# One operation for the three scalings of an attention step, and a newly drawn order of work

## The chip, the cores and the metric

The kernel runs on one core of one Trainium2 chip. The metric is the device time of one execution in microseconds (us), from launch to end. The core has five engines that run side by side: TensorE (PE in the rows; its weight loads are PEld), VectorE (DVE), ScalarE (ACT), GpSimd (POOL) and SyncE (SP), which issues the transfers. SBUF is the on-chip working memory, PSUM the memory into which TensorE writes.

## The reference, cut to what matters

Three stages follow one another: an attention over a sliding window of 64 positions, a feed-forward stage with a rational activation, and a second, bilinear feed-forward stage.

```python
# q, k, v: (4, 8, 576, 64)
scores = scale * np.matmul(q, k.transpose(0, 1, 3, 2))
scores = np.where((rel >= 0) & (rel < 64), scores, -1000000000.0)
attn = np.exp(scores - scores.max(-1, keepdims=True))
attn = attn / (np.sum(attn, axis=-1, keepdims=True) + 1e-09)   # the scaling
x = np.matmul(attn, v)            # then reshaped to (2304, 512)
h = x @ w_in                      # (512, 2048)
g = (a0 + a1*h + a2*h*h + a3*h*h*h) / (1 + |b0|*|h| + |b1|*h*h + 1e-6)
x = g @ w_out                     # (2048, 512)
out = ((x @ w1) * (x @ w2)) @ w3 @ w_out2
```

## The kernel before, in words

**The attention.** The work is cut into 48 steps. A step is one pair of heads and 192 query positions, in three windows of 64 positions; its scores fill a tile `sm` of 128 partitions by 3 x 128 elements. Two consecutive steps are a pair (the function `attn`) and share a small tile `st` of 24 columns, in which the row minima, the row sums, the sums plus 1e-9 and their reciprocals of both steps stand, three columns for each step. One step is this chain: the scores on TensorE (`S`, L555); for each of the three windows a masked row minimum on VectorE (`tr`, L558) and an exponential with row sum on ScalarE (`e`, L564); once for the pair, the sum plus 1e-9 on GpSimd (`rs`, L498) and the reciprocal on VectorE (`rc`, L501); for each window the scaling of the 128 x 128 block by its reciprocals (`nm`, on ScalarE at L569 or on GpSimd at L571); three transposes on TensorE (`T`, L576); one copy out of PSUM on ScalarE (`ac`, L581); the product with v on TensorE (`O`, L508); and once for the pair two operations that split the result into two tiles for the next stage (`xh` on ScalarE, L518; `xl` on VectorE, L521).

**The first feed-forward stage** takes blocks of 384 tokens. Its products are L646 (`hp`) and L723 (`acc`), its activation runs on ScalarE and VectorE, and the last multiplication of it, `lo` (L717), can run on VectorE or, for the first three blocks, on GpSimd. The weights arrive as 64-bit numbers and are converted by five operations each, four on VectorE (L408, L411, L414, L424) and one on ScalarE (L421). The second feed-forward stage (L1023, L1150 and L879) has no part in the attention's work.

**What sets the order.** No loop emits the instructions. Every operation is registered with the engines it may run on and a cost in us for each (`op`), with what it comes after and which buffers it uses; the costs are numbers written by hand. The planner (`order`, L72 to L216) lays all operations of the kernel out in one schedule by these costs and due times, 17 times over, and keeps the shortest one. The due times of the first round are shifted by random numbers from a seed (L198). Where an operation names two engines, the planner takes one of them. It lets an operation on GpSimd and one of VectorE that is marked `port=True` never overlap in its schedule. The order of the shortest schedule is the order of instructions on every engine and of the transfers in SyncE's queue. So a cost or the seed can move any instruction of the kernel.

Of the 48 steps, the first 16 may scale on GpSimd; the other 32 scale on ScalarE.

Of the kernel before, what the change touches and what calls it, by code (L numbers as in the profile page):

```python
# [3 lines left out]

# [36 lines left out]
class Plan:  # L41
# [30 lines left out]
    def order(self, rounds=16):  # L72
# [122 lines left out]

        first = dues(base)
        preds = buffers(lambda a: first[a] if ops[a]["turn"] is None else ops[a]["turn"])
        rng = Random(55)  # L198
        due = [d + rng.gauss(0.0, 0.5) for d in dues(preds)]
        best = None  # L200
        for r in range(rounds + 1):
# [18 lines left out]
def body(ctx: ExitStack, tc: tile.TileContext, qkv, qk0, w_in, w_out, a, b, w1, w2, w3t, wo2, out):  # L220
# [260 lines left out]
    def attn(pair):  # L481


        i0 = 2 * pair
        u, p0 = STEPS[i0]
        s = u % NU
        j, o = u // 2, (u % 2) * U
        early = i0 < 2 * NP
        y = units.setdefault(u, [{} for _ in range(NP // 2)])[p0 // 2]

        def rows(f):
            return y["st"][:, 6 * f:6 * f + 6]

        def col(f, k, m):
            return y["st"][:, 6 * f + NW * k + m:6 * f + NW * k + m + 1]

        def rs(_):
            nc.gpsimd.tensor_scalar(out=rows(2), in0=rows(1), scalar1=1e-9, scalar2=1.0, op0=ADD, op1=MUL)  # L498

        def rc(_):  # L500
            dve.reciprocal(rows(3), rows(2))  # L501

        def O(k, y=y):
            if k == 0:
                y["op"] = psum.tile([P, 2, U], F32, tag="at", bufs=2, name="op")
            for w in range(NW):
                for h in (slice(0, 64), slice(64, P)):
                    nc.tensor.matmul(y["op"][h, k, w * W_:(w + 1) * W_], y["v", k][:, w, h], y["ac", k][:, w, h], start=True, stop=True)  # L508
            if u % 2 == 0 and k == 0 and y is units[u][0]:
                xh[j], xl[j] = xtiles(XSLOT[j], "x")  # L510

        def OO(_):
            for y in units[u]:
                for k in range(2):
                    O(k, y)

        def xh_(_):
            act(xh[j][:, p0:p0 + 2, o:o + U], y["op"], cp)  # L518

        def xl_(_):  # L520
            dve.tensor_tensor(out=xl[j][:, p0:p0 + 2, o:o + U], in0=y["op"], in1=xh[j][:, p0:p0 + 2, o:o + U], op=SUB)  # L521

        def step(k):
            i, p = i0 + k, p0 + k

            tags = (f"acc{i % 2}", f"acc{2 + i % 2}") if early else ("at", "at")
            x = {}

            def load(_):
                x["k"] = ap_.tile([P, U + W_], F32, tag="k", bufs=rings["k"], name="k")  # L530
                if i < THIN:
                    if k == 0:
                        y["q"] = ap_.tile([P, 2 * U], F32, tag="q", bufs=rings["q"], name="q")
                        nc.sync.dma_start(out=y["q"], in_=qk0[u, p0 // 2])
                    x["q"] = y["q"].rearrange("d (k w n) -> d k w n", k=2, w=NW)[:, k]
                    nc.sync.dma_start(out=x["k"], in_=qkv[u, p, :, 2 * U:3 * U + W_])
                    return
                q = ap_.tile([P, 2 * U], F32, tag="q", bufs=rings["q"], name="q")
                x["q"] = q.rearrange("d (w n) -> d w n", w=NW)
                nc.sync.dma_start(out=q, in_=qkv[u, p, :, 0:2 * U])  # L540
                nc.sync.dma_start(out=x["k"], in_=qkv[u, p, :, 2 * U:3 * U + W_])

            def loadv(_):
                y["v", k] = ap_.tile([P, NW, P], F32, tag="v", bufs=rings["v"], name="v")
                nc.sync.dma_start(out=y["v", k], in_=qkv[u, p, :, 3 * U + W_:].rearrange("r (w d) -> r w d", w=NW))


            def S_(_):
                x["sp"] = sp = psum.tile([P, NW, P], F32, tag=tags[0], bufs=rings[tags[0]], name="sp")
                x["sm"] = ap_.tile([P, NW, P], F32, tag="sm", bufs=rings["sm"], name="sm")  # L550
                if k == 0:
                    y["st"] = ap_.tile([P, 24], F32, tag="st", bufs=rings["st"], name="st")
                for w in range(NW):
                    for h in (slice(0, 64), slice(64, P)) if i < THIN else (slice(0, P),):
                        nc.tensor.matmul(sp[h, w, :], x["q"][h, w], x["k"][h, w * W_:w * W_ + P], start=True, stop=True)  # L555

            def tr(m):
                dve.tensor_tensor_reduce(  # L558
                    out=x["sm"][:, m, :], in0=x["sp"][:, m, :], in1=mask0 if s == 0 and m == 0 else mask, scale=-SCALE, scalar=3.0e38,
                    op0=ADD, op1=ALU.min, accum_out=col(0, k, m),  # L560
                )

            def e(m):
                act(x["sm"][:, m, :], x["sm"][:, m, :], AF.Exp, bias=col(0, k, m), scale=-1.0, accum_out=col(1, k, m))  # L564

            def nm(m, e):
                r, t = col(3, k, m), x["sm"][:, m, :]
                if e == "A":
                    act(t, t, cp, scale=r)  # L569
                else:  # L570
                    nc.gpsimd.tensor_scalar(out=t, in0=t, scalar1=r, scalar2=1.0, op0=MUL, op1=MUL)  # L571

            def T(_):
                x["tp"] = tp = psum.tile([P, NW, P], F32, tag=tags[1], bufs=rings[tags[1]], name="tp")
                for w in range(NW):
                    nc.tensor.transpose(tp[:, w, :], x["sm"][:, w, :], idn)  # L576

            def ac(_):

                y["ac", k] = x["sm"]  # L580
                act(y["ac", k], x["tp"], cp)  # L581

            kb_, vb, qb, mb, sp, tp = ("k", i), ("v", i), ("q", i0 if i < THIN else i), ("sm", i), (tags[0], ("S", i)), (tags[1], ("T", i))
            thin = i < THIN
            op(("load", i), (("D", (0.48 if k else 1.12) if thin else 1.1),), load, after=[("load", i0)] if thin and k else (), new=(kb_,) if thin and k else (kb_, qb), uses=(qb,) if thin and k else (), tail=2.2)
            op(("loadv", i), (("D", 0.66),), loadv, after=(("load", i),), new=(vb,), tail=2.2)
            pe(("S", i), S_, TS, after=[("load", i)] + [("S", i - 1)] * k, new=(sp, mb) if k else (sp, mb, sb), uses=(kb_, qb, sb) if k else (kb_, qb))
            for m in range(NW):
                op(("tr", i, m), (("V", 0.21),), lambda _, m=m: tr(m), after=(("S", i),), uses=(sp, mb, sb))
                op(("e", i, m), (("A", 0.39),), lambda _, m=m: e(m), after=(("tr", i, m),), uses=(mb, sb))  # L590
            for m in range(NW):
                op(("nm", i, m), (("A", 0.32), ("P", 0.52)) if i < 16 else (("A", 0.32),), lambda e, m=m: nm(m, e), after=(("rc", i0),), uses=(sb, mb))
            pe(("T", i), T, TT, after=[("nm", i, m) for m in range(NW)], new=(tp,), uses=(mb,))
            op(("ac", i), (("A", 0.45),), ac, after=(("T", i),), uses=(tp, mb))
            if early:
                xn = i == 0
                pe(("O", i), lambda _: O(k), TO[k], after=[("ac", i), ("loadv", i)] + [("O", i - 1)] * k, new=() if k else (ob, xb) if xn else (ob,), uses=(mb, vb, ob, xb) if k else (mb, vb) if xn else (mb, vb, xb))

        sb, ob, xb = ("st", i0), ("at", ("O", i0)), (f"x{XSLOT[j]}", j)
        op(("rs", i0), (("P", 0.12),), rs, after=[("e", i0 + k, m) for k in range(2) for m in range(NW)], uses=(sb,))  # L600
        op(("rc", i0), (("V", 0.12),), rc, after=(("rs", i0),), uses=(sb,))
        for k in range(2):
            step(k)
        if not early and p0:
            four, xn = range(i0 - 2, i0 + 2), u % 2 == 0
            new = (("at", ("O", i0 - 2)), ob) + ((xb,) if xn else ())
            pe(("O", i0 + 1), OO, TOO, after=[(w, i) for i in four for w in ("ac", "loadv")], new=new, uses=tuple((b, i) for i in four for b in ("sm", "v")) + (() if xn else (xb,)))
        op(("xh", i0), (("A", 0.40),), xh_, after=(("O", (i0 if early else i0 // NP * NP + 2) + 1),), uses=(ob, xb))
        op(("xl", i0), (("V", 0.43),), xl_, after=(("xh", i0),), uses=(ob, xb))


    kept, AGAIN = {}, "again"
# [21 lines left out]
    def chunks(c0):  # L634
# [121 lines left out]
        op(("w", c0), (("V", 0.87),), w, port=True, after=(("hi", c0),), uses=(b["qa"], b["g"]))  # L756
        op(("d", c0), (("V", 0.87 if estrin else 0.93),), d, port=True, after=(("w", c0),), uses=(b["u"], b["qa"]))
        for m in range(2):
            engines = (("V", 0.47), ("P", 0.97))[:2 if j < G else 1]
            op(("lo", c0 + m), engines, lambda e, m=m: lo(m, e), port=True, after=(("d", c0),), uses=(b["u"], b["r"], b["g"]))  # L760
        for m in range(2):
            c, f = c0 + m, f0 + m
# [497 lines left out]
```

## Time and profile before

| what | us |
|---|---|
| median of 3 runs | 814.37 (813.99 to 817.33) |
| the profiled execution | 815.26 |
| span of its instructions | 813.4 |
| around the span | 1.9 |

A page of the profile has the busy time of each engine, a line of the span in 40 slices, the chain of work that ended last, and groups of instructions by source line. Tables by stretch give the busy time of each engine between two times; a table of waits says which engine's idle time ended with which other instruction; a timeline lists single instructions. The longest instruction of an engine is not its cost alone: an instruction that cannot get at its data shows the time as its own.

### The profile page before, as it was taken

The numbers are of one execution on the slowest core, as the hardware profiler recorded it, in microseconds if no ns is written. First come the engines' busy times: TensorE is split into PE (matmuls) and PEld (weight loads), VectorE is DVE, ScalarE is ACT, GpSimd is POOL, SyncE is SP. The second block draws the span as 40 slices with busy tenths as digits, with TensorE's granted clock in tenths as the row PEclk, the third lists the DMA queues.
The fourth block names the chain that finished last, engine by engine and source line by source line (L and its number), as shares of the span: only waits on it lengthen the run. The fifth ranks groups of instructions, "written<-read, shape, count | busy, mean of one in ns | idle before, by whom it ended". The sixth has DMA issues, their size and how long they took to land.

```text
span 813.4 us, 14381 instructions
## 1 busy us (share of the span) xinstructions
PE 789.3 (97%) x5112; PEld 767.6 (94%) x5112; DVE 734.0 (90%) x1445; ACT 562.6 (69%) x1263; POOL 47.0 (6%) x72
## 2 busy tenths in 40 slices
PE   5779999999999999999999999999999999999998
PEld 4579999999999999999999999889999999999998
DVE  6999999999999899999999999899999788837854
ACT  6998996787889878788877676267465456544433
POOL 2223210000001200000000000000000000000000
PEclk9999999999999999999999999999999999999999
DMA  8883473234438666455443632678978775136402
GB/s 279 296 280 116 118 228 117 98 97 144 149 120 269 215 207 208 161 204 184 145 140 137 241 120 85 213 255 280 330 243 268 240 269 177 63 116 213 160 1 77
DMA packets 62951, 147.74 MB, mean 182 GB/s; under 512 B 7072, under 2 KB 35744, under 8 KB 62880
## 3 DMA queue, kind: packets, MB, share of 16 engines
q1 hardware_dynamic: 62880, 146.83, 53.4%
q8 instruction: 40, 0.66, 0.3%
q14 instruction: 31, 0.25, 0.1%
HBM read 114.30 MB, written 32.51 MB: 180 GB/s over the span
## 4 chain that ended last, share of the span: by engine, by line
PE 85%; DVE 9%; DMA 3%; ACT 2%; issue 1%; POOL 0%; SPq 0%; DVEq 0%; POOLq 0%
PE acc L723 23%; PE hp L646 22%; PE pb L1023 8%; PE wp L879 5%; PE pc L1023 5%; PE pa L1023 5%; PE pb L1150 5%; PE pc L1150 3%; PE pa L1150 3%; PE sp L555 3%; PE op L508 2%; PE tp L576 1%; DVE wt L414 1%; DVE wt L411 1%; DMA wc<-kw 1%
## 5 line engine op out<-in xcount | busy, mean ns | idle before, releaser
L646 PE MATMUL hp<-x,wc 128*128 128x384 f32 x1152 | 218.9, 338 | 2.8 <-DVE u L674 2.1
L723 PE MATMUL acc<-g,wc 128*128 128x384 f32 x1152 | 219.4, 338 | 1.2 <-DVE g L717 1.1
L646 PEld LDWEIGHTS hp<-x,wc 128*128 128x128 f32 x1152 | 199.6, 188 | 5.2 <-DVE u L674 2.9
L723 PEld LDWEIGHTS acc<-g,wc 128*128 128x128 f32 x1152 | 199.6, 188 | 3.6 <-DVE g L717 2.4
L1023 PE MATMUL pb<-xb,wc 128*128 128x384 f32 x432 | 84.2, 334 | 0.0
L1023 PEld LDWEIGHTS pb<-xb,wc 128*128 128x128 f32 x432 | 75.7, 188 | 0.0
L687 ACT ACTIVATE r<-qa,cq 128x768 f32<-128x768 f32 x48 | 45.3, 943 | 41.0 <-DVE qa L683 23.1
L668 ACT ACTIVATE u<-hp,ca 128x384 f32<-128x384 f32 x96 | 65.0, 677 | 6.7 <-PE hp L646 6.4
L663 ACT ACTIVATE qa<-hp,cb 128x384 f32<-128x384 f32 x96 | 55.8, 581 | 13.1 <-PE hp L646 10.9
L564 ACT ACTIVATE sm<-sm,st 128x128 f32<-128x128 f32 x144 | 56.1, 399 | 9.1 <-DVE st L558 8.9
L1112 ACT ACTIVATE rt<-prod 128x768 fp32r<-128x768 f32 x42 | 35.5, 846 | 32.2 <-PE pb L1150 9.7
L1023 PE MATMUL pa<-xb,wc 128*128 128x384 f32 x288 | 56.9, 335 | 0.5 <-DMA wc<-kw 0.5
L1023 PE MATMUL pc<-xb,wc 128*128 128x384 f32 x288 | 55.9, 334 | 0.0
L555 PE MATMUL sp<-k,q 64*64 64x128 f32 (+1 forms) x384 | 42.9, 309 | 12.8 <-DMA k<-in_qkv 8.5
L1115 DVE TENSOR_TENSOR rt<-prod,rt 128x768 fp32r<-128x768 f32 x42 | 40.0, 955 | 16.5 <-ACT rt L1112 16.0
L658 ACT ACTIVATE h<-hp 128x384 f32<-128x384 f32 x96 | 47.1, 490 | 9.6 <-PE hp L646 7.9
L555 PEld LDWEIGHTS sp<-k,q 64*64 64x64 f32 (+1 forms) x384 | 39.0, 183 | 15.1 <-issue 8.3
L1023 PEld LDWEIGHTS pa<-xb,wc 128*128 128x128 f32 x288 | 50.5, 188 | 1.0 <-DMA wc<-kw 0.8
L1023 PEld LDWEIGHTS pc<-xb,wc 128*128 128x128 f32 x288 | 50.4, 188 | 0.0
L683 DVE SCALAR_TENSOR_TENSOR qa<-h,cab,qa 128x768 f32<-128x768 f32 x48 | 48.4, 1008 | 1.2 <-ACT qa L663 1.1
L411 DVE SCALAR_TENSOR_TENSOR wt<-ws,wt 128x512 uint32<-128x512 uint32 x72 | 49.0, 682 | 0.3
L414 DVE SCALAR_TENSOR_TENSOR wt<-ws,wt 128x512 uint32<-128x512 uint32 x72 | 49.0, 683 | 0.1
(86 smaller groups left out, 1376.9 us busy)
## 6 DMA issues: line engine op xcount, KB each, us to landing
wc<-kw SPq DMA_DIRECT2D x48, 512.0 KB, 4.9
bs<-kb SPq DMA_DIRECT2D x24, 512.0 KB, 4.3
v<-in_qkv SPq DMA_DIRECT2D x48, 192.0 KB, 3.9
ws<-in_w_in SPq DMA_DIRECT2D x16, 512.0 KB, 4.8
ws<-in_w_out SPq DMA_DIRECT2D x16, 512.0 KB, 4.8
ws<-in_w SPq DMA_DIRECT2D x16, 512.0 KB, 4.0
kw<-ws SPq DMA_DIRECT2D x16, 512.0 KB, 3.5
ws<-in_w3t SPq DMA_DIRECT2D x16, 512.0 KB, 4.1
```

The lines of the kernel that those rows point to most:

```text
L411: stt(out=x["b"], in0=x["st"][:, :, 0], scalar=29, in1=x["b"], op0=ALU.logical_shift_right, op1=ALU.bitwise_or)
L414: stt(out=x["b"], in0=x["st"][:, :, 1], scalar=0xC0000000, in1=x["b"], op0=ALU.bitwise_and, op1=ALU.bitwise_or)
L555: nc.tensor.matmul(sp[h, w, :], x["q"][h, w], x["k"][h, w * W_:w * W_ + P], start=True, stop=True)
L564: act(x["sm"][:, m, :], x["sm"][:, m, :], AF.Exp, bias=col(0, k, m), scale=-1.0, accum_out=col(1, k, m))
L646: nc.tensor.matmul(x["hp", m], win[f0 + m][:, s_, kk * P:(kk + 1) * P], (xh, xl)[m_][xk][:, kk, :], start=(kk == 0 and i == 0), stop=(kk = ...
L658: act(x["h2"][:, m, :], x["hp", m], AF.Square)
L663: act(x["qa"][:, m, :], x["hp", m], AF.Abs, scale=b0)
L668: act(x["u"][:, m, :], x["hp", m], AF.Identity, scale=a3, bias=a2)
L683: stt(out=x["qa"], in0=x["h2"], scalar=b1, in1=x["qa"], op0=MUL, op1=ADD)
L723: nc.tensor.matmul(accs[j, part, n], wout[f0 + m][:, s_, n * P:(n + 1) * P], x["g"][:, m_, m, :], start=(first and i == 0), stop=(last and ...
L1023: nc.tensor.matmul(x[m], sws[u, n, i0][:, s_, (c0 + k) * P:(c0 + k + 1) * P], t[:, m_, k, :], start=(first and k == 0 and i == 0), stop=(k ...
L1150: nc.tensor.matmul(x[m, n], w[:, s_, (c + n) * P:(c + n + 1) * P], rts[u, b, r][:, m_, k, :], start=(first and r == 0 and k == 0 and i == ...
```

## The change

In the first 16 steps the three scalings `nm` of a step become one operation `nms`. On GpSimd it is a single multiplication of the whole tile by the three reciprocals, each spread over its 128 columns; on ScalarE it is the same three instructions as before, one behind the other, but taken or left as a whole. Some costs that the planner reckons with are changed as well (`rs`, `ac`, `xh`, `xl`, and `lo` on GpSimd), and the seed.

```diff
-        rng = Random(55)
+        rng = Random(19)
...
+            def nms(e):
+                if e == "A":
+                    for m in range(NW):
+                        nm(m, e)
+                else:
+                    r = y["st"][:, 18 + NW * k:18 + NW * (k + 1)].unsqueeze(2).to_broadcast([P, NW, P])
+                    nc.gpsimd.tensor_tensor(out=x["sm"], in0=x["sm"], in1=r, op=MUL)
...
-            for m in range(NW):
-                op(("nm", i, m), (("A", 0.32), ("P", 0.52)) if i < 16 else (("A", 0.32),), lambda e, m=m: nm(m, e), after=(("rc", i0),), uses=(sb, mb))
-            pe(("T", i), T, TT, after=[("nm", i, m) for m in range(NW)], new=(tp,), uses=(mb,))
-            op(("ac", i), (("A", 0.45),), ac, after=(("T", i),), uses=(tp, mb))
+            whole = i < 2 * 2 * NP
+            for m in range(0 if whole else NW):
+                op(("nm", i, m), (("A", 0.32),), lambda e, m=m: nm(m, e), after=(("rc", i0),), uses=(sb, mb))
+            if whole:
+                op(("nm", i), (("A", 0.9), ("P", 1.25)), nms, after=(("rc", i0),), uses=(sb, mb))
+            pe(("T", i), T, TT, after=[("nm", i)] if whole else [("nm", i, m) for m in range(NW)], new=(tp,), uses=(mb,))
+            op(("ac", i), (("A", 0.43),), ac, after=(("T", i),), uses=(tp, mb))
...
-        op(("rs", i0), (("P", 0.12),), rs, after=[("e", i0 + k, m) for k in range(2) for m in range(NW)], uses=(sb,))
+        op(("rs", i0), (("P", 0.3),), rs, after=[("e", i0 + k, m) for k in range(2) for m in range(NW)], uses=(sb,))
...
-        op(("xh", i0), (("A", 0.40),), xh_, after=(("O", (i0 if early else i0 // NP * NP + 2) + 1),), uses=(ob, xb))
-        op(("xl", i0), (("V", 0.43),), xl_, after=(("xh", i0),), uses=(ob, xb))
+        op(("xh", i0), (("A", 0.43),), xh_, after=(("O", (i0 if early else i0 // NP * NP + 2) + 1),), uses=(ob, xb))
+        op(("xl", i0), (("V", 0.465),), xl_, after=(("xh", i0),), uses=(ob, xb))
...
-            engines = (("V", 0.47), ("P", 0.97))[:2 if j < G else 1]
+            engines = (("V", 0.47), ("P", 1.4))[:2 if j < G else 1]
```

## Rows read from the trace of the kernel before

**Rows 1.** The page, busy time of each engine, share of the span, instructions:

```profile
PE 789.3 (97%) x5112; PEld 767.6 (94%) x5112; DVE 734.0 (90%) x1445; ACT 562.6 (69%) x1263; POOL 47.0 (6%) x72
```

**Rows 2.** Table by stretch: busy us of each engine, granted clock, DMA share, GB/s:

```profile
0.00:14.00 14.00, 5.46 (x47) 4.72 (x49) 7.86 (x32) 6.30 (x22) 2.27 (x13) 1.00 0.79 262
14.00:76.00 62.00, 51.75 (x517) 45.19 (x516) 58.98 (x169) 55.82 (x174) 21.29 (x31) 0.97 0.72 246
76.00:470.00 394.00, 392.66 (x2666) 386.73 (x2663) 388.48 (x773) 320.92 (x755) 23.44 (x29) 1.00 0.50 167
470.00:814.00 344.00, 339.44 (x1895) 330.98 (x1893) 278.67 (x473) 179.58 (x316) 0.00 (x0) 1.00 0.54 183
```

**Rows 3.** Waits in 14:76: us in total, times, longest us:

```profile
PEld op L508 <- ACT sm L581: 3.2, 5, 1.1
PEld hp L646 <- DVE u L674: 2.4, 1, 2.4
PEld sp L555 <- DVE x L521: 2.4, 1, 2.4
...
PEld tp L576 <- POOL sm L571: 1.4, 2, 0.9
...
PEld tp L576 <- ACT sm L569: 0.6, 1, 0.6
```

**Rows 4.** Groups by line, 14:76: count, busy us, mean ns, idle before:

```profile
L571 POOL TENSOR_SCALAR sm<-sm,st 128x128 f32<-128x128 f32 x19 | 12.5, 670 | 7.3 <-DVE st L501 7.3
L717 POOL TENSOR_TENSOR g<-u,r 128x384 fp32r<-128x384 f32 x5 | 6.9, 1397 | 10.5 <-ACT x L518 6.1 <-DVE u L713 4.5
...
L569 ACT ACTIVATE sm<-sm,st 128x128 f32<-128x128 f32 x29 | 9.8, 392 | 0.7 <-DVE st L501 0.7
...
L424 DVE TENSOR_TENSOR wc<-wt,wc 128x512 fp32r<-128x512 f32 x13 | 8.9, 691 | 0.3 <-ACT wc L421 0.3
```

**Rows 5.** Timeline, first and last of the eight pairs: reciprocal and scalings:

```profile
13.79 0.18 DVE L501 RECIPROCAL st<-st 128x6 f32<-128x6 f32 x1
...
14.06 1.06 POOL L571 TENSOR_SCALAR sm<-sm,st 128x128 f32<-128x128 f32 x2 [0.90 <-DVE st L501]
14.46 1.26 ACT L569 ACTIVATE sm<-sm,st 128x128 f32<-128x128 f32 x4
...
70.27 0.18 DVE L501 RECIPROCAL st<-st 128x6 f32<-128x6 f32 x1
...
70.49 1.28 ACT L569 ACTIVATE sm<-sm,st 128x128 f32<-128x128 f32 x4
70.61 2.79 POOL L571 TENSOR_SCALAR sm<-sm,st 128x128 f32<-128x128 f32 x2 [1.53 <-DVE st L501]
```

**Rows 6.** Timeline of GpSimd, single instructions in narrow windows:

```profile
30.47 0.37 POOL L571 TENSOR_SCALAR sm<-sm,st 128x128 f32<-128x128 f32 x1
...
71.82 1.58 POOL L571 TENSOR_SCALAR sm<-sm,st 128x128 f32<-128x128 f32 x1
...
51.69 1.64 POOL L717 TENSOR_TENSOR g<-u,r 128x384 fp32r<-128x384 f32 x1 [6.07 <-ACT x L518]
...
53.29 1.00 POOL L717 TENSOR_TENSOR g<-u,r 128x384 fp32r<-128x384 f32 x1
```

**Rows 7.** Timeline at 71 us and 51 us, VectorE beside these:

```profile
72.30 0.95 DVE L707 SCALAR_TENSOR_TENSOR qa<-qa,g 128x768 f32<-128x768 f32 x1
...
51.47 1.01 DVE L683 SCALAR_TENSOR_TENSOR qa<-h,cab,qa 128x768 f32<-128x768 f32 x1
```

**Rows 8.** Timeline at 256 us, VectorE and GpSimd:

```profile
256.38 1.20 DVE L424 TENSOR_TENSOR ws<-wt,ws 128x512 fp32r<-128x512 f32 x1
...
256.00 1.03 POOL L717 TENSOR_TENSOR g<-u,r 128x384 fp32r<-128x384 f32 x1 [7.94 <-DVE u L711]
```

**Rows 9.** Table by stretch around 53 us, columns as in rows 2:

```profile
50.50:53.00 2.50, 0.25 (x11) 0.11 (x5) 2.50 (x5) 2.08 (x5) 1.31 (x1) 0.99 1.01 353
53.00:57.00 4.00, 4.00 (x29) 3.67 (x30) 3.81 (x18) 2.54 (x9) 1.29 (x2) 0.58 0.45 146
```

More of the change, by code (lines that the diff above doesn't have):

```diff
@@ L2 @@
 from heapq import heappop, heappush
+from random import Random
 from random import Random
```

## The prediction

> **What bounds the kernel now.** I read the page first, then a table by stretch, then the waits of the stretch that the change touches, then groups and single instructions of the three engines that the scalings meet. The page says that TensorE is busy for 789.3 of 813.4 us [rows 1], so 24.1 us are all that any better order could take out of its idle time. The table shows where they lie: from 76 to 470 us it idles 394.00 - 392.66 = 1.3 us and from 470 us on 4.6 us, of which about 0.6 us is the rounding of the stretch past the span's end [rows 2]. The rest, 8.5 us before 14 us and 62.00 - 51.75 = 10.25 us between 14 and 76 us, is the start [rows 2]. The first scaling comes at 14.06 us [rows 5], so the change itself can only act on the second stretch and what follows.
>
> In 14 to 76 us the engines stand close together: VectorE is busy 58.98 of 62 us (95%), ScalarE 55.82 (90%), TensorE 51.75 (83%), the transfers have a share of 0.72, and GpSimd has 21.29 us [rows 2]. So VectorE is nearest to the bound, ScalarE next, and GpSimd has room. TensorE's waits there end on four kinds of work: the copy `ac` on ScalarE (3.2 us), two single waits on VectorE of 2.4 us each, a scaling on GpSimd (1.4 us) and one on ScalarE (0.6 us) [rows 3]. The scalings as such thus explain 1.4 + 0.6 = 2.0 us.
>
> **What the change removes and adds.** Sixteen steps have 48 scalings. In the profile 19 ran on GpSimd (12.5 us, 670 ns each) and 29 on ScalarE (9.8 us busy, 392 ns each, overlapping to 1.28 / 4 = 0.32 us when back to back) [rows 4, 5]. They become 16 operations, each wholly on one engine.
>
> How many go to which engine is decided by the planner, and no row shows it. Both steps of a pair become ready with the same reciprocal, and there are two engines, so I take 8 and 8. The ends are 0 and 16 on GpSimd.
>
> *One operation on GpSimd.* The nearest row is L717, also a product of two tiles of 128 x 384: 1.00 us with little beside it, 1.64 us where VectorE was in the middle of a 1.01 us operation when it began, 1397 ns in the mean of this stretch [rows 4, 6, 7]. The old operation shows the same: 0.37 us alone, 1.58 us with a 0.95 us operation of VectorE inside it [rows 6, 7]. So GpSimd waits out VectorE, and I price the new one at 1.0 us plus that wait, 1.4 us in all, with 1.0 and 2.1 (1.0 plus one 1.0 us operation and a little) as ends. Three old ones cost 3 x 0.37 = 1.1 us alone and 3 x 0.67 = 2.0 us as they ran. That the second input is three numbers spread over 128 columns I cost at nothing: as many elements are read as in L717. GpSimd then has 8 x 1.4 = 11.2 us where it had 12.5; its time is not the point.
>
> The Trainium skill, "GPSIMD Engine Reference", section 4.1 (Engine selection), speaks against the trade: operations with two inputs run at about half of VectorE's rate there, those with one input at nearly the full rate. Section 3.1 of that page has 2.6 against 1.03 cycles an element; by that ratio three times 0.37 us would turn into about 2.8 us (an estimate from the page), a pair would end 0.7 us later than before instead of earlier, and the sum below would be about -0.3 us instead of -2.3. The trace doesn't agree: 384 elements with two inputs took 1.00 us, 128 with one took 0.37 us [rows 6], 2.6 and 2.9 ns an element.
>
> *The path to the transposes.* A transpose of a step waits for all its scalings. From the end of the reciprocal to the last scaling of a pair the first pair took 15.72 - 13.97 = 1.75 us and the last 73.40 - 70.45 = 2.95 us [rows 5]; over all eight pairs read that way it is 18.1 us, 2.26 in the mean. Afterwards ScalarE needs 3 x 0.32 = 0.96 us for its step and GpSimd 1.4 us, each after a start of 0.1 to 0.2 us, together about 1.6 us: 0.7 us less for a pair, 5.6 us for eight. Only 2.0 us of the 18.1 made TensorE wait, so the gain lies between nothing and 2.0 us; I take the 1.4 us that ended on GpSimd.
>
> *ScalarE.* Eight steps cost 8 x 0.96 = 7.7 us where 9.8 were, 2.1 us less. Most of that hides behind VectorE, which is busier. What shows is the 3.2 us wait for `ac`; I take 0.9 us, between nothing and 2.1.
>
> *The hand-written costs* change no instruction. `lo` on GpSimd at 1.4 instead of 0.97 agrees better with 1397 ns [rows 4] and may send some of the five `lo` of this stretch to VectorE; that is work for the fuller engine, and relief from its waits. I cost it at nothing, with half a microsecond a piece to either side. No transfer is added or taken away, but SyncE's queue is written in the planner's order too, so every load can move. That and the seed's effect can't be costed from the trace; the rivals bound them.
>
> The sum is -1.4 - 0.9 = -2.3 us: 815.26 becomes 813.0 for the profiled execution, which stood 0.9 above the median, and 814.37 becomes 812.1.
>
> **The rivals.** About 0.5%, 4.1 us, is what a measurement of this kernel tells from no change, so faster is below 810.3 and slower above 818.4.
>
> *A. The sum holds and the new order is neither better nor worse.* 812.1, in its own range 810.3 to 816. For it: after 76 us TensorE idles for under 6 us, so another order has little to find there, and before 14 us nothing changes in kind. Chance 0.46.
>
> *B. The new order removes stalls of TensorE at the start.* The wait on `xl` before 53 us is 2.4 us; and behind the idle time the granted clock is 0.58 in the mean of the next 4.0 us [rows 9], part of it at the lower of the two levels, which costs 4.0 x 0.42 = 1.7 us. Without that stall: 2.3 + 2.4 + 1.7 = 6.4 us less, 808.0. With the other wait of 2.4 us gone as well, 805.6. For it: single waits depend on the order alone and both lie where the order is drawn anew. Against it: VectorE at 95% leaves only 3.0 us idle in the stretch, so its work must be sorted, not shortened. Chance 0.36.
>
> *C. GpSimd holds up VectorE.* At 256 us an operation of VectorE that takes 691 ns elsewhere took 1.20 us while GpSimd's 1.03 us operation ran [rows 4, 8]: 0.51 us lost. An old scaling could hold it for at most 0.37 us, the new one for 1.0. If all 16 went to GpSimd and each cost VectorE 0.51 us, that is 8.2 us on the engine nearest to the bound: 812.1 + 8.2 = 820.3, slower. It decides from 6.3 / 0.51, thirteen such meetings; eight give 816.2, no change. The Trainium skill, "GPSIMD Engine Reference", section 8 (Key points), names this: GpSimd shares its way into SBUF with VectorE and contends with operations of two SBUF inputs; the 1.20 us agree. Against it: the planner keeps the two apart in its schedule, and the other rows show GpSimd as the one that waits. Chance 0.08.
>
> *D. The new order adds stalls.* Two more like that of 53 us, 4.1 us each, give 812.1 + 8.2 = 820.3. Chance 0.07.
>
> *E. The planner leaves the steps on ScalarE,* so that the change doesn't do what it says: 48 x 0.32 = 15.4 us there instead of 9.8, 5.6 us more on an engine that idles for 6.2. Between 812 and 820. Chance 0.03.
>
> **How the numbers follow.** Faster 0.36 (B), same 0.46 (A), slower 0.18 (C, D and E). The predicted time is A's, 812.1. The range goes from 805.5, B with both waits gone, to 820, just short of C and D at their full price; beyond lie an order that finds more than B, and the worse ends of C and D, together about 2 in 10.
>
> **What would show it.** In the new profile L571 is gone, and about eight products of 128 x 384 of `sm` with `st` run on GpSimd with a mean of 1.4 us and a minimum of 1.0; ScalarE's scalings before 76 us number about 24. From reciprocal to last scaling a pair takes some 1.6 us, and transposes wait less than 2.0 us for scalings. TensorE's idle time between 14 and 76 us is near 8 us for A, under 5 for B, over 14 for D; for C single operations of VectorE at L411, L414 or L424 stand above 1 us. The prediction is wrong if the stretch behind 76 us is longer or shorter by more than 2 us, if the single operation takes over 2.1 us, or if a new idle stretch of TensorE pulls the clock down once more.

## The result

The changed kernel takes 819.98 us in the median of 7 runs (819.11 to 821.35), the kernel before 813.99 in 7 runs beside them (813.28 to 817.33): a ratio of 1.0059, 95% interval 1.0041 to 1.0077. It is slower: by the ratio 4.8 us, and the medians stand 6.0 us apart. The profiled execution took 819.71 us with a span of 817.9; before it was 815.26 and 813.4, so the two traces differ by 4.5 us.

The table by stretch of the changed kernel, with the columns of [rows 2]:

```profile
0.00:14.00 14.00, 4.46 (x38) 3.72 (x40) 6.96 (x28) 5.40 (x17) 2.22 (x13) 1.00 0.74 242
14.00:76.00 62.00, 52.46 (x518) 45.83 (x519) 57.33 (x167) 54.80 (x174) 13.34 (x19) 0.92 0.75 245
76.00:470.00 394.00, 391.92 (x2650) 385.72 (x2649) 386.31 (x766) 320.08 (x753) 28.34 (x35) 1.00 0.48 164
470.00:818.00 348.00, 342.44 (x1912) 333.87 (x1910) 283.16 (x481) 184.08 (x320) 0.00 (x0) 1.00 0.55 186
```

The counts in parentheses locate the loss. TensorE executes the same 5112 matmuls in both kernels. Behind 470 us the changed kernel still has 1912 of them to do where 1895 were left before [rows 2]. They are 17 matmuls, and 24 of them take 4.16 us when nothing holds them up (the chain of the changed kernel):

```profile
189.09 4.16 PE hp L658 x24
```

So it is 17 x 0.173 = 2.9 us behind at 470 us, and loses the rest of the 4.5 us later. The busy times behind 470 us say the same, 342.44 us against 339.44. (It is one trace's number: two other traces of this order have 1901 and 1908 matmuls left there.)

Divided at 76 us, the 4.5 us have two halves. At 76 us the changed kernel has 391.92 + 342.44 = 734.4 us of TensorE's work left, where 732.1 were left before [rows 2], 2.3 us more. Behind 76 us TensorE idles 7.5 us and not 5.3, 2.2 us more. Up to 76 us it idles hardly more than before: 9.5 us against 8.5 in the first 14 us, and 9.5 against 10.3 from 14 to 76 us. What is behind at 76 us is therefore for the most part matmuls that took longer (see the clock below). The 1.0 us of the first stretch is not tied to the order: in the run below that moves one transfer at 612 us, with the same order up to there, TensorE idles 14.00 - 5.91 = 8.1 us:

```profile
0.00:14.00 14.00, 5.91 (x48) 4.77 (x48) 8.46 (x33) 6.90 (x23) 2.83 (x14) 1.00 0.80 267
```

TensorE's waits behind 76 us, of the changed kernel (us in total, times, longest):

```profile
PE pa L1035 <- DMA wc<-kw: 1.6, 1, 1.6
PE hp L658 <- DVE u L686: 1.4, 3, 0.7
PE hp L658 <- DVE x L522: 0.3, 1, 0.3
PE acc L735 <- ACT sm L565: 0.3, 1, 0.3
```

They sum to 3.6 us. The 1.6 us end on a weight transfer at 625 us. In the kernel before, the waits of this stretch summed to 1.6 us:

```profile
PE acc L723 <- DVE g L717: 1.1, 2, 0.8
PE pa L1023 <- DMA wc<-kw: 0.5, 1, 0.5
```

Around the scalings the groups by line from 14 to 76 us, as in [rows 4], became:

```profile
L580 POOL TENSOR_TENSOR sm<-sm,st 128x384 f32<-128x384 f32 x7 | 7.3, 1043 | 6.3 <-DVE st L502 4.9 <-PE op L509 1.5
L729 POOL TENSOR_TENSOR g<-u,r 128x384 fp32r<-128x384 f32 x4 | 4.0, 1006 | 13.3 <-DVE u L725 13.2
...
L570 ACT ACTIVATE sm<-sm,st 128x128 f32<-128x128 f32 x27 | 8.7, 390 | 2.0 <-DVE st L502 2.0
...
L425 DVE TENSOR_TENSOR wc<-wt,wc 128x512 fp32r<-128x512 f32 x13 | 9.2, 710 | 0.0
```

Seven steps scale on GpSimd and nine on ScalarE (27 = 9 x 3). One operation takes 1043 ns. And TensorE's waits from 14 to 76 us, which answer to [rows 3]:

```profile
PEld hp L658 <- DVE u L686: 4.3, 2, 2.5
...
PEld tp L585 <- ACT sm L570: 2.5, 4, 2.0
PEld sp L556 <- DVE x L522: 2.1, 1, 2.1
PEld op L509 <- ACT sm L590: 2.0, 3, 0.8
```

No transpose waits for GpSimd any more. Instead the transposes wait 2.5 us for scalings on ScalarE, where both engines together gave 2.0 us before [rows 3]; and the waits on VectorE's L686 (L674 before) are 4.3 us instead of 2.4.

### The profile page after: what moved, and what is told of

Read it like the earlier page. It is cut to its first block, busy times and chain, and to the rows that moved or that the text cites. A ratio compares the mean times of both kernels' runs of the same rounds, so it can differ in the third digit from the quotient of the medians.

```text
span 817.9 us, 14355 instructions
## 1 busy us (share of the span) xinstructions
PE 791.3 (97%) x5112; PEld 769.1 (94%) x5112; DVE 733.8 (90%) x1439; ACT 564.4 (69%) x1261; POOL 43.9 (5%) x66
## 4 chain that ended last, share of the span: by engine, by line
PE 77%; DVE 16%; ACT 4%; DMA 2%; issue 1%; SPq 0%; ACTq 0%; DVEq 0%
PE hp L658 17%; PE acc L735 17%; PE pb L1035 9%; PE pa L1035 6%; PE pc L1035 6%; PE wp L891 5%; PE pb L1162 5%; PE pc L1162 3%; PE pa L1162 3%; PE sp L556 3%; DVE u L725 2%; DVE sm L559 2%; DVE u L683 2%; DVE u L686 1%; DVE qa L695 1%; PE op L509 1%
## 5 line engine op out<-in xcount | busy, mean ns | idle before, releaser
L412 DVE SCALAR_TENSOR_TENSOR wt<-ws,wt 128x512 uint32<-128x512 uint32 x72 | 50.2, 700 | 0.2
L415 DVE SCALAR_TENSOR_TENSOR wt<-ws,wt 128x512 uint32<-128x512 uint32 x72 | 49.1, 684 | 0.1
```

Source lines behind the costliest of these rows:

```text
L412: stt(out=x["b"], in0=x["st"][:, :, 0], scalar=29, in1=x["b"], op0=ALU.logical_shift_right, op1=ALU.bitwise_or)
L415: stt(out=x["b"], in0=x["st"][:, :, 1], scalar=0xC0000000, in1=x["b"], op0=ALU.bitwise_and, op1=ALU.bitwise_or)
```

## The experiments

Theory 1 is that the order drawn anew costs the time (rival D of the prediction); theory 2 that the single operation on GpSimd does, by holding VectorE up (rival C); theory 3 that the new hand-written costs lead to worse orders; theory 4 that VectorE's total work sets the start. Each ratio is against the kernel before on the same chip, whose median there was 814.8 to 815.9 us.

**The operation with the order kept.** Two kernels take the planner out of the question. The first keeps the changed kernel's order and goes back to three scalings on GpSimd:

```diff
-                    r = y["st"][:, 18 + NW * k:18 + NW * (k + 1)].unsqueeze(2).to_broadcast([P, NW, P])
-                    nc.gpsimd.tensor_tensor(out=x["sm"], in0=x["sm"], in1=r, op=MUL)
+                    for m in range(NW):
+                        nc.gpsimd.tensor_scalar(out=x["sm"][:, m, :], in0=x["sm"][:, m, :], scalar1=col(3, k, m), scalar2=1.0, op0=MUL, op1=MUL)
```

> The changed kernel's order kept instruction for instruction, but each of the seven spread products on GpSimd is written as three scalings of 128x128 in its place. Theory 1, the new order is what costs (rival D): the time stays within 2 us of the changed kernel, 818 to 822. Theory 2, the single operation holds VectorE up (rival C): most of the 6 us comes back, 814 to 817, and the VectorE operations of over 0.9 us at the lines of the weight conversion are gone.

Measured: 819.5 us, ratio 1.0057 (1.0040 to 1.0074), the same as the changed kernel. The second keeps the order of before and puts in the single operation (`merged[i]` is the spread product of step i, defined as in the change):

```diff
-        for o in plan.order():
+        made = plan.order()
+        on = {i: [o["engine"] for o in made if o["key"][:2] == ("nm", i)].count("P") for i in range(16)}
+        one = {i + (on[i + 1] >= on[i]) for i in range(0, 16, 2)}
+        for o in made:
+            i = o["key"][1] if o["key"][0] == "nm" else None
+            if i in one:
+                if merged[i]:
+                    merged[i](None)
+                merged[i] = None
+            elif i in on:
+                o["fn"]("A")
+            elif o["fn"]:
...
```

> The order of the kernel before, but of each pair's first 16 steps one is scaled by a single spread product on GpSimd, where its first scaling on GpSimd stood, and the other by three on ScalarE. Theory 1 (order): within 2 us of the kernel before, 812 to 816. Theory 2 (the operation): slower by 3 to 6 us, 817 to 820, with VectorE operations prolonged by about half a microsecond in the first 76 us.

Measured: 816.17 us, ratio 1.0011 (1.0000 to 1.0021). So in either order the operation is worth nothing that shows (in the old one between nothing and 1.7 us of loss), and the order carries the loss. Groups on GpSimd from 14 to 76 us, first of the changed order with three scalings, then of the old order with one:

```profile
L580 POOL TENSOR_SCALAR sm<-sm,st 128x128 f32<-128x128 f32 x21 | 14.2, 690 | 6.2 <-DVE st L502 6.2
```

```profile
L575 POOL TENSOR_TENSOR sm<-sm,st 128x384 f32<-128x384 f32 x8 | 9.5, 1182 | 7.5 <-DVE st L501 7.5
```

Three scalings take 3 x 690 = 2.07 us of GpSimd, one takes 1.04 to 1.18 us, and the end doesn't care.

**The parts, each with its own order.** Only the registration of the single operation, with the old costs and the old seed; and only the five costs.

> The single operation is registered as in the changed kernel, the other costs and the seed stay those of before; the order is drawn anew. Theory 1 (order): anything from 812 to 820, since it is another draw. Theory 2 (the operation): 817 to 821. Theory 3 (the new costs worsen the order): as before, 812 to 816.

> Only the five costs are changed, with the seed and the scalings of before. Theory 1 (order): another draw, 812 to 820. Theory 2 (the operation): as before, 812 to 816. Theory 3 (the new costs worsen the order): 817 to 821.

Measured: 820.37 us, ratio 1.0064 (1.0049 to 1.0079), and 823.92 us, 1.0106 (1.0088 to 1.0124). Both parts lose, though the one has nothing of the other. Theories 2 and 3 each forbid one of the two. The draw of theory 1 forbids neither, but both lie above the 820 that was put down as its end, so its spread was taken too small; 823.92 is above theory 3's end as well.

**Other draws.** Each is the kernel of the table's first two columns with another seed, in the third.

> The kernel before with nothing changed but the seed, 19 instead of 55. Theory 1a (the order before was an uncommonly good draw, and any other draw loses): 817 to 823. Theory 1b (only the operations' new costs or the merged scaling make worse orders): within 2 us of the kernel before, 812 to 817.

> The kernel before with seed 22. Theory 1a (the order before was an uncommonly good draw): 816 to 823. Theory 1b: 812 to 817.

> The changed kernel with seed 20 instead of 19. Theory 1a (it is the draw, not the change): somewhere from 813 to 823, not tied to 820. Theory 1b (the new costs make worse orders): 818 to 823.

> The merged scaling alone with the old costs, seed 44. Theory 1a (the draw): 813 to 823, as likely below as above the 820.4 of seed 55. Theory 1b (the merged scaling makes worse orders): 818 to 823.

> The merged scaling with the costs of before and seed 269, the shortest schedule among some thousand seeds by the planner's own reckoning. If shorter schedules run shorter on the chip: 811 to 815, at or below the kernel before. If the reckoning says nothing of the chip: 813 to 822.

> Only the five costs changed, three scalings as before, seed 83, the shortest schedule of a hundred seeds by the planner's reckoning with these costs. Theory 1a (the draw): 813 to 818, well below the 823.9 of seed 55. Theory 3 (the new costs worsen every order): 819 to 824.

> The changed kernel with seed 8, a third draw of its order. Theory 1a (the draw alone decides): 813 to 823, with no leaning. Theory 3 (the new costs lean towards worse orders): 816 to 823.

> The kernel before with seed 30, a fourth draw of its order. Theory 1a: 813 to 823. Theory 3: 813 to 818.

> The merged scaling with the costs of before and seed 0, a fourth draw of that kind. Theory 1a (the draw alone): 813 to 823. Theory 3 (the new costs lean towards worse orders, the merged scaling doesn't): 813 to 818.

> Only the five costs changed, seed 70, a third draw of that kind. Theory 1a (the draw alone): 813 to 823. Theory 3 (the new costs lean towards worse orders): 817 to 824.

| scalings | costs | seed | ratio | 95% interval |
|---|---|---|---|---|
| three | old | 55 (before) | 1 | |
| three | old | 19 | 1.0024 | 1.0004 to 1.0043 |
| three | old | 22 | 1.0002 | 0.9984 to 1.0019 |
| three | old | 30 | 1.0030 | 1.0013 to 1.0048 |
| one | old | 55 | 1.0064 | 1.0049 to 1.0079 |
| one | old | 44 | 0.9992 | 0.9975 to 1.0009 |
| one | old | 269 | 1.0042 | 1.0025 to 1.0058 |
| one | old | 0 | 1.0036 | 1.0021 to 1.0051 |
| three | new | 55 | 1.0106 | 1.0088 to 1.0124 |
| three | new | 83 | 1.0048 | 1.0036 to 1.0060 |
| three | new | 70 | 1.0031 | 1.0019 to 1.0042 |
| one | new | 19 (the change) | 1.0059 | 1.0041 to 1.0077 |
| one | new | 20 | 1.0027 | 1.0008 to 1.0045 |
| one | new | 8 | 1.0034 | 1.0022 to 1.0047 |

Thirteen orders other than the one before: the mean is 1.0038, some 3 us, and none is faster beyond its interval. With seed 44 the single operation is as fast as the kernel before, so it doesn't make orders bad as such. With the new costs the six stand at 1.0051 in the mean, the other seven at 1.0027; without the one at 1.0106 it is 1.0040. The two groups overlap, so theory 3 stays open: the 0.24% between them may belong to the costs or to the draw. That any other draw loses (theory 1a as first put) falls with seeds 22 and 44. The order before is among the best three of the fourteen; whether seed 55 had been picked for that is not on record. Its own kernel, drawn anew with three other seeds, stands at 1.0019 in the mean, 1.5 us. Seed 269 was the shortest of some thousand schedules by the planner's own reckoning, seed 83 the shortest of a hundred; at 1.0042 and 1.0048 both lost all the same.

**Moving single late instructions.** In the changed order VectorE's second product of the first chunk (L686) stands behind a conversion, six row minima and a longer product, and TensorE waits 2.3 us for it at 45 us. It was moved directly behind the first product; in a second kernel four such were, with (0, 4, 20, 34) in place of (0,):

```diff
+        for c in (0,):
+            v = next(o for o in made if o["key"] == ("v", c))
+            made.remove(v)
+            made.insert(next(n for n, o in enumerate(made) if o["key"] == ("uh", c)) + 1, v)
...
```

> The changed kernel's order with one instruction moved: the second product of the first chunk's activation on VectorE stands directly behind the first product instead of behind a conversion, six row minima and a longer product. Theory 1 (single late instructions at the start make TensorE wait, and the clock falls behind the wait): the wait of 2.3 us at 45 us and the stretch at half clock behind it go, and the end comes 2 to 4 us sooner, 816 to 818. Theory 4 (VectorE's total work sets the start, so a wait taken away comes back at the next place): the end moves by less than 1 us, 819 to 821.

> The same move for the four such instructions for which TensorE waits at 45, 69, 115 and 145 us (2.3, 1.4, 0.5 and 0.7 us). Theory 1: the four waits go and the end comes 4 to 6 us sooner, 814 to 816. Theory 4: less than 1.5 us, 818.5 to 821.

Measured: 818.46 us, 1.0054 (1.0041 to 1.0066), and 821.20 us, 1.0077 (1.0060 to 1.0093): no gain from one, and if anything a loss from four. The timeline of TensorE with the one moved shows why:

```profile
42.20 2.37 PE L658 MATMUL hp<-x,wc 128*128 128x384 f32 x12
46.59 2.16 PE L658 MATMUL hp<-x,wc 128*128 128x384 f32 x6 [2.02 <-DVE u L686]
```

The products now begin at 42.20 us without a wait, and the next chunk's wait 2.02 us for the next L686. The wait has moved by one chunk.

**Taking work from VectorE.** That looked like theory 4, so in the changed order five conversions leave out one operation each, and with it the sign bits of their weights:

```diff
         def b2_(_):
+            if key in (("win", 3), ("win", 4), ("win", 5), ("wout", 1), ("wout", 2)):
+                return
```

> The changed kernel, and five of the operations of 0.69 us on VectorE in the first 40 us are left out (the sign bits of five weight tiles are lost). Theory 4 (VectorE's work sets the start): the end comes 2 to 3 us sooner, 817 to 818. Theory 1 (single late instructions elsewhere, or ScalarE and the transfers): less than 1 us.

Measured: 820.53 us, 1.0057 (1.0036 to 1.0077). VectorE's busy time from 14 to 76 us fell, the end didn't come sooner:

```profile
14.00:76.00 62.00, 52.68 (x521) 45.84 (x522) 54.87 (x161) 54.99 (x172) 12.91 (x19) 0.92 0.73 247
```

54.87 us instead of 57.33, with ScalarE now the fuller engine (54.99). Theory 4 is not borne out: the middle moved by 0.2 us, though the two intervals leave room for some 2 us. ScalarE's sum was not tried alone.

**The late transfer.** At 625 us the changed kernel waits for a weight tile whose issue stands in SyncE's queue behind three loads of tokens. It was moved ahead of them:

```diff
+        late = next(o for o in made if o["key"] == ("sw", 1, 3, 0))
+        made.remove(late)
+        made.insert(next(n for n, o in enumerate(made) if o["key"] == ("xl2", 2, "B12")), late)
...
```

> The changed kernel's order with one transfer moved: a weight tile of the second feed-forward stage is issued ahead of three loads of tokens instead of behind them, so that it should land several us sooner than the time at which TensorE waits 1.6 us for it (625 us). Theory D (new order, waits at several places): the end comes 1 to 1.6 us sooner, 818.4 to 819. If VectorE's backlog sets the end there as well: within 0.5 us.

SyncE's queue in the changed kernel, and with the transfer moved:

```profile
612.17 0.32 SPq L996 DMA_DIRECT2D bs<-kb  x1
615.32 3.19 SPq L962 DMA_DIRECT2D xf<-x2d  x3
618.61 0.42 SPq L992 DMA_DIRECT2D wc<-kw  x1
```

```profile
612.13 0.32 SPq L996 DMA_DIRECT2D bs<-kb  x1
612.54 0.38 SPq L992 DMA_DIRECT2D wc<-kw  x1
615.27 3.20 SPq L962 DMA_DIRECT2D xf<-x2d  x3
```

The load goes out at 612.54 us and no longer at 618.61, and TensorE's wait for a transfer behind 470 us is gone; what is left there is this:

```profile
PE pa L1035 <- DVE xb L969: 0.5, 1, 0.5
```

Measured: 818.25 us, 1.0033 (1.0019 to 1.0047). That is 0.26% below the changed kernel's 1.0059, 2.1 us, in size what the wait of 1.6 us says. The two intervals still touch; but the four other kernels above that keep this order and a wait of 1.0 us or more on the transfer (three scalings, one instruction moved, four moved, five operations left out) stand at 1.0054 to 1.0077.

## Why the prediction was wrong

Two steps failed, both in rival A: that the sum holds, and that the new order is neither better nor worse.

**The sum: its pieces held in size, its terms did not arrive.** *One operation on GpSimd* was priced at 1.4 us, with 1.0 to 2.1 as ends; it took 1.04 us in the mean. Seven of sixteen went there, eight were assumed. *The path to the transposes* was to shorten from 2.26 to 1.6 us for a pair; read the same way the eight pairs of the changed kernel sum to 11.2 us, 1.40 each. *ScalarE* was to do 24 scalings in the stretch; it did 27. But where the prediction's sum has -2.3 us, the same single operation in the old order gave a ratio of 1.0011, about +0.9 us, and in the new order three scalings instead of one gave 1.0057 against 1.0059. The trace of the old order with the single operation shows both terms; TensorE's waits from 14 to 76 us there:

```profile
PEld op L508 <- ACT sm L587: 3.0, 5, 1.1
...
PEld tp L582 <- ACT sm L569: 2.8, 2, 1.6
```

No transpose waits for GpSimd, but they wait 2.8 us for scalings on ScalarE, where both engines together gave 2.0 us [rows 3]: the term of -1.4 us came out as +0.8. The wait for `ac`, from which 0.9 us were to come, is 3.0 us instead of 3.2. The same happened in the changed kernel (the 2.5 us above), and there a wait taken away at one place was met at the next (the moved L686).

**The order: the larger step.** "The new order is neither better nor worse" failed, and with it the place where the seed's effect was left out of the sum because it could not be costed. An order drawn anew costs this kernel 0.38% in the mean of thirteen, the change among them, 3.1 us, and -0.1 to +1.1% in the single case. By these the centre should have stood about 3 us above the time before (1.5 us by the three draws of the old kernel alone), and faster should have had less than the 0.36 it was given: none of thirteen came out faster. The reason given for A, that little idle time is left behind 76 us, bounds what an order can gain there and not what it can lose. In the worst draw (only the costs new, 1.0106) TensorE waits 7.9 us behind 76 us, where 1.6 us were. The largest of these waits:

```profile
PE acc L723 <- DVE g L717: 4.2, 3, 2.0
PE hp L646 <- DVE u L674: 1.8, 3, 1.2
PE sp L555 <- DVE x L521: 1.3, 1, 1.3
```

That 819.98 us lies below the range's upper end of 820 is luck: that end stood for C and D at 8.2 us each, and neither came in that form. Two of the signs named for a wrong prediction did come: the stretch behind 76 us is 4.5 us longer, and idle stretches pull the clock down again.

**Rival D was the right kind, its form another.** It asked for two more stalls of 4.1 us and for over 14 us of idle time of TensorE from 14 to 76 us; there were 9.5 us, near the 8 of A. What came were several small ones behind 76 us: 1.4 + 0.3 + 0.3 us where 1.1 us were, and the transfer at 625 us with 1.1 us more. The run that moved the transfer makes its share likely, 1.0033 against 1.0054 to 1.0077 in the five kernels of this order that keep the wait. In the start the waits changed their places and hardly their sum (19.1 us of idle time up to 76 us, 18.8 before). No run brought back what is lost there: neither moving one or four late instructions, nor taking VectorE's work away. What sets it among VectorE, ScalarE, TensorE and the transfers, which are busy for 0.75 to 0.92 of that stretch, stays open.

**Rival C's mechanism exists and does not decide.** At 18 us in the changed kernel, GpSimd and VectorE:

```profile
18.69 1.17 POOL L580 TENSOR_TENSOR sm<-sm,st 128x384 f32<-128x384 f32 x1 [0.88 <-DVE st L502]
```

```profile
18.52 0.65 DVE L415 SCALAR_TENSOR_TENSOR wt<-ws,wt 128x512 uint32<-128x512 uint32 x1
19.09 1.32 DVE L412 SCALAR_TENSOR_TENSOR wt<-ws,wt 128x512 uint32<-128x512 uint32 x1
```

GpSimd's operation begins while L415 runs and takes 1.17 us where its shortest take 0.83. L412 begins while GpSimd's runs and ends 0.55 us behind it: 1.32 us where L412's like takes 0.69. It happened to three more operations of VectorE:

```profile
37.65 1.17 DVE L425 TENSOR_TENSOR wc<-wt,wc 128x512 fp32r<-128x512 f32 x1
...
46.91 1.12 DVE L412 SCALAR_TENSOR_TENSOR wt<-ws,wt 128x512 uint32<-128x512 uint32 x1
...
60.80 0.94 DVE L409 TENSOR_SCALAR wt<-ws 128x512 uint32<-128x512 uint32 x1
```

The four take 0.69, 0.69, 0.69 and 0.42 us elsewhere, so they lose 2.1 us in all. The Trainium skill, "GPSIMD Engine Reference", section 8 (Key points), names such contention with VectorE's operations of two SBUF inputs or in a two-port mode. The trace agrees for the three that read two tiles, L412 twice and L425; in what mode the fourth, with one input, runs no row shows. But with three scalings in the same order no conversion on VectorE stood above 0.86 us, and the time was the same; and five operations less on VectorE moved the end by less than the measurement tells.

**The clock** fell behind TensorE's waits again, longer than in [rows 9]. Table by stretch of the changed kernel around two of them:

```profile
23.50:28.00 4.50, 2.14 (x24) 1.16 (x20) 4.50 (x20) 3.95 (x16) 1.11 (x2) 1.00 0.98 310
28.00:34.80 6.80, 6.15 (x54) 4.87 (x54) 5.54 (x16) 5.86 (x21) 1.30 (x2) 0.50 0.88 255
42.00:45.00 3.00, 0.78 (x16) 0.53 (x10) 2.86 (x16) 3.00 (x12) 0.00 (x0) 1.00 0.91 262
45.00:48.50 3.50, 3.44 (x11) 3.45 (x12) 3.50 (x8) 3.50 (x10) 1.03 (x2) 0.51 0.86 261
```

After stretches with TensorE busy for 2.14 of 4.50 and 0.78 of 3.00 us it runs at the lower level, 1.2 GHz. From 14 to 76 us the mean is 0.92 instead of 0.97. The same 96 products `hp` up to 76 us then take longer, first before, then in the changed kernel:

```profile
L646 PE MATMUL hp<-x,wc 128*128 128x384 f32 x96 | 19.7, 348 | 2.8 <-DVE u L674 2.1 <-DVE x L521 0.7
```

```profile
L658 PE MATMUL hp<-x,wc 128*128 128x384 f32 x96 | 21.6, 368 | 4.0 <-DVE u L686 3.7 <-DVE x L522 0.3
```

All 5112 matmuls together are busy for 791.3 us instead of 789.3 [rows 1]. In the trace of the same order with three scalings, at the same mean of 0.92, the 96 take 20.0 us and all of them 789.9, so what falls into the slow stretches differs from run to run: 0.6 to 2.0 us in these traces. The clock alone does not make the loss either: with the single operation and seed 44 the mean is 0.92 in the same stretch, and the time is that of before.

```profile
14.00:76.00 62.00, 52.32 (x511) 44.97 (x508) 57.74 (x165) 55.27 (x171) 14.97 (x19) 0.92 0.72 240
```

## What to carry to other kernels

Where a planner writes the order, an edit of one operation redraws all of it; cost the redrawing by itself, from a few other seeds of the old kernel, before crediting or blaming the operation. (Here they would have given 1.5 us and not the 4.8 of the change, but the right sign.) To test the operation, keep the old order and exchange it in place. And where several engines and the transfers are busy nearly all the time, an instruction that is late for one wait can hide the next one: here moving it moved the wait.

## What the runs showed that was not expected

The product with a spread operand is faster than L717's with a full second operand: its shortest cases took 0.83 us where L717 alone took 1.00 us [rows 6], on the same 128 x 384 elements. That the spreading is the reason is not shown, since L717 also writes another type (fp32r) into another tile.

```profile
37.44 0.83 POOL L580 TENSOR_TENSOR sm<-sm,st 128x384 f32<-128x384 f32 x1 [0.53 <-DVE st L502]
```

An operation of only six columns on GpSimd (`rs`, the sum plus 1e-9 of a pair) takes 0.20 us:

```profile
28.91 0.20 POOL L499 TENSOR_SCALAR st<-st 128x6 f32<-128x6 f32 x1 [3.03 <-ACT sm L565]
```

So a good part of the 0.37 us that one old scaling of 128 columns took alone is not its elements'. The prediction set 2.9 ns an element for the old operation against 2.6 for one with two inputs. A straight line from 6 to 128 columns gives 0.17 us / 122 = 1.4 ns for the old operation, one from 0.20 us at 6 columns to 0.83 us at 384 gives 0.63 us / 378 = 1.7 ns for the new one (estimates from these rows). By them the new operation is not cheaper for an element. It is cheaper than three, 0.83 against 3 x 0.37 = 1.1 us, as it would be if a part that does not depend on the columns is paid once and not three times. The dearer price of 2.8 us that the prediction names beside its own did not come (1.04 us), and the -0.3 us given with it, whose working is not shown, falls with it.
